# High parts first in every split product, and a new order of all steps (chunked attention with memory keys and a spatial-gating MLP, one core)

## The chip, the cores and the metric

The kernel runs on one core of one Trainium2 chip. The metric is device time in microseconds (us). The kernel before took 388.06 us, the median of three runs between 385.65 and 389.63 us.

Engines are named as in the profile: PE (matrix multiply; PEld is its weight load), DVE (vector), ACT (scalar functions), POOL (GpSimd), SP (the queue from which all loads and stores of data are issued).

## The reference

Attention in chunks of 32 tokens, each with 16 tokens to its left, 8 to its right and 8 memory keys; then an MLP whose gate mixes the tokens of a sequence:

```
for c in range(768 // 32):
    k_full = concat(mem_k, k[:, :, max(0, 32*c-16) : min(768, 32*c+32+8)])
    v_full = the same of v
    a = softmax(q_c @ k_full.T / 8);  out_c = a @ v_full
x = out, heads joined                       # 4 x 768 x 512
h = gelu(x @ w_in)                          # 4 x 768 x 1024
u, v = h[..., :512], h[..., 512:]
v_n = (v - mean) / sqrt(var + 1e-6) * g_ln
v_s = einsum('ts,bsd->btd', w_sg, v_n) + b_sg
result = x + (u * v_s) @ w_out
```

All inputs and the result are float32.

## The kernel before, in words

**Tiles.** Each of the 4 batches has 6 tiles of 128 tokens, 24 tiles in all, counted here from 0. Tiles 0, 1 and 2 are the first half of batch 0; a half of a batch has 384 tokens.

**Split products.** Every large operand is held as a high part (rounded to fp32r) and a low part (what is left). A product is made of three passes over its parts: low of one side with high of the other, high with low, high with high. `HL` (line 390) gives the order of the passes and `product` (line 392) issues them. A product's operands come in parts from other engines, so a pass can begin when its own parts are there.

**Steps.** The whole program is cut into named steps, each on one engine, and the long string `ORDER` (lines 32 to 80) lists all of them in the order in which they are recorded. Every engine runs its own steps in that order and waits where data or a buffer is missing; nothing overtakes. A star at a name takes the step's second engine. What the names mean, with tile u, batch b, half h, column block j:

- `q`, `k`, `v` + u: loads of a tile's queries, keys, values (SP); two buffers for q and k, three for v. `ri..`, `ro..`: loads of the pieces of w_in and w_out; `g` + two digits: loads of the pieces of w_sg.
- `d3`, `d2`, `d5`, `d6`, `d8`, `d9` + piece: turn 64-bit weights to float32 and split them (ACT, DVE, DVE, DVE, ACT, and POOL, DVE or ACT). `Xi1.` are PE steps that subtract the high part for four pieces of w_in. `ga`, `gb`: high and low part of w_sg (ACT; POOL or DVE).
- `S` u scores (PE), `mx`, `sb` largest and subtraction (DVE), `ex` exponential (ACT), `z` zeroes keys outside (POOL), `sm`, `sr` sum and reciprocal (DVE), `nm` normalisation (DVE or POOL), `T` transposes (PE), `p` their copy out of PSUM (ACT or DVE), `A` attention times values (PE), `xc`, `xh`, `xl` copy, high part and low part of the tile's result x (ACT, ACT, DVE or POOL).
- `V` b tile: x times the v half of w_in (PE, 12 matmuls of 512 columns), `v1` to `v9`: gelu, the layer norm and the split (the normalisation `v7` waits for the power `v6` on POOL). `U` b h j: x times the u half (12 matmuls of 384 columns), `u1` its gelu. `W`: the mix over tokens (18 matmuls), `w1` to `w4`: scale, gate, split. `O`: times w_out (12 matmuls), `o1` the sum with x, `out` the store.
- `zz` n: n matmuls on the identity, which compute nothing that is used.

A score step and a value step have 64 small matmuls each in the trace, with as many weight loads.

**What a reader needs from the code.** In before, the lines on which the change rests are these; the functions that issue them stand below:

```
HL = ((1, 0), (0, 1), (0, 0))
for a, c in HL:
    for lhs, rhs in parts:
        eng.matmul(ps, lhs(a), rhs(c), start=(k == 0), stop=(k == n - 1))
```

Part 0 is the high part, part 1 the low part; a is the part of the left operand, c of the right one.

## Time and profile before

| what | value |
|---|---|
| runs | 388.06 us median (385.65, 388.06, 389.63) |
| the profiled execution | 387.39 us, of which its span is 385.6 us |
| PE busy | 375.7 us, 97% of the span |
| DVE busy | 216.4 us, 56% |
| ACT busy | 154.1 us, 40% |
| POOL busy | 80.9 us, 21% |
| data moved | 43.95 MB |

The span goes from the first to the last instruction of the program; 1.8 us of the profiled execution lie around it. Busy is time in which an engine has an instruction in work. PE's matmuls overlap each other a little, so the length of a step is better read from the chain of waits, where each piece begins when the one before it ends.

### The profile page before, as it was taken

The numbers are of one execution on the slowest core, as the hardware profiler recorded it, in microseconds if no ns is written. First come the engines' busy times: TensorE is split into PE (matmuls) and PEld (weight loads), VectorE is DVE, ScalarE is ACT, GpSimd is POOL, SyncE is SP. The second block draws the span as 40 slices with busy tenths as digits, with TensorE's granted clock in tenths as the row PEclk, the third lists the DMA queues.
The fourth block names the chain that finished last, engine by engine and source line by source line (L and its number), as shares of the span: only waits on it lengthen the run. The fifth ranks groups of instructions, "written<-read, shape, count | busy, mean of one in ns | idle before, by whom it ended". The sixth has DMA issues, their size and how long they took to land.

```text
span 385.6 us, 10848 instructions
## 1 busy us (share of the span) xinstructions
PE 375.7 (97%) x4832; PEld 345.7 (90%) x4832; DVE 216.4 (56%) x404; ACT 154.1 (40%) x261; POOL 80.9 (21%) x100
## 2 busy tenths in 40 slices
PE   7979999999999999999999999999999999999996
PEld 3547988899999988899999989899999988999996
DVE  3799999999966365565345432531542414525522
ACT  3587799666531363463014341531210232511100
POOL 1003175223522201302005301420012133410010
PEclk9989999999999999999999999999999999999999
DMA  8999776756535246112002230000001110000022
GB/s 285 407 397 346 240 253 207 255 194 218 191 114 174 93 140 214 45 36 77 0 2 76 85 129 23 22 2 0 0 2 61 63 41 0 2 0 2 6 78 82
DMA packets 19150, 43.95 MB, mean 114 GB/s; under 512 B 2592, under 2 KB 8224, under 8 KB 19104
## 3 DMA queue, kind: packets, MB, share of 16 engines
q1 hardware_dynamic: 19104, 43.26, 31.8%
q8 instruction: 38, 0.62, 0.7%
q14 instruction: 8, 0.07, 0.1%
HBM read 36.96 MB, written 6.29 MB: 112 GB/s over the span
## 4 chain that ended last, share of the span: by engine, by line
PE 90%; DMA 3%; DVE 3%; ACT 2%; issue 1%; SPq 0%; ACTq 0%
PE mmd L92 22%; PE mmb L92 21%; PE mmc L92 19%; PE mma L92 19%; PE av L92 5%; PE s L92 4%; DMA ka<-in_ks 2%; DMA vb<-in_vs 1%; DVE w_sg_lo L92 0%; ACT L92 0%; SPq L92 0%; DVE pt L92 0%; ACT w_in_hi L92 0%; ACT pt L92 0%; ACT w_sg_hi L92 0%
## 5 line engine op out<-in xcount | busy, mean ns | idle before, releaser
L92 ACT ACT_TABLE_LOAD x20 | 25.7, 1283 | 3.6 <-DVE w_sg_lo L92 2.4
L92 DVE SCALAR_TENSOR_TENSOR mmd<-mmd,g_all,b_all 128x384 f32<-128x384 f32 x9 | 5.6, 620 | 15.7 <-PE mmd L92 15.7
L92 DVE SCALAR_TENSOR_TENSOR mmc<-mmc,g_all,b_all 128x384 f32<-128x384 f32 x8 | 5.0, 625 | 14.3 <-PE mmc L92 14.3
L92 PEld LDWEIGHTS av<-pt,vb 64*64 64x64 f32 x512 | 8.3, 134 | 4.2 <-issue 2.9
L92 PE MATMUL av<-pt,vb 64*64 64x32 f32 x512 | 9.3, 220 | 2.9 <-issue 2.1
L92 PEld LDWEIGHTS s<-kb,qb 64*32 64x32 f32 x768 | 8.7, 109 | 3.6 <-issue 1.7
L92 DVE SCALAR_TENSOR_TENSOR mmb<-mmb,g_all,b_all 128x384 f32<-128x384 f32 x9 | 5.6, 619 | 11.3 <-PE mmb L92 11.3
L92 PE MATMUL s<-ka,qa 64*32 64x64 f32 x768 | 10.5, 232 | 1.3 <-DMA ka<-in_ks 1.3
L92 PE MATMUL mmd<-w_in_hi,paira 128*128 128x512 f32 x40 | 11.7, 415 | 0.0
L92 PE MATMUL s<-kb,qb 64*32 64x64 f32 x768 | 10.8, 231 | 0.8 <-issue 0.8
L92 PEld LDWEIGHTS s<-ka,qa 64*32 64x32 f32 x768 | 8.7, 108 | 3.1 <-issue 2.0
L92 PE MATMUL mma<-ident 128*128 128x512 f32 (+1 forms) x16 | 9.9, 768 | 1.4 <-POOL mhalf L92 1.4
L92 PE MATMUL mmb<-w_in_hi,paira 128*128 128x512 f32 x40 | 11.0, 397 | 0.0
L92 PE MATMUL mmd<-w_in_hi,pairb 128*128 128x512 f32 x40 | 11.0, 396 | 0.0
L92 POOL TENSOR_TENSOR rsa<-rsa,mhalf 128x1 f32<-128x1 f32 x8 | 4.4, 551 | 28.2 <-DVE rsa L92 28.2
L92 DVE TENSOR_REDUCE mxa<-s 128x8 f32<-128x512 f32 x8 | 5.5, 684 | 8.2 <-PE s L92 8.2
L92 PEld LDWEIGHTS av<-pt,va 64*64 64x64 f32 x512 | 8.2, 135 | 1.8 <-issue 1.0
L92 POOL TENSOR_TENSOR paira<-xc,paira 128x512 fp32r<-128x512 f32 x4 | 5.5, 1410 | 19.8 <-ACT paira L92 19.8
L92 PEld LDWEIGHTS mmd<-w_in_hi,paira 128*128 128x128 f32 x40 | 7.8, 201 | 1.7
L92 PEld LDWEIGHTS av<-pt,vc 64*64 64x64 f32 x512 | 8.2, 135 | 1.3 <-issue 1.3
L92 PE MATMUL mma<-pairb,w_in_hi 128*128 128x384 f32 x48 | 9.3, 336 | 0.0
L92 PE MATMUL av<-pt,va 64*64 64x32 f32 x512 | 9.0, 220 | 0.1
(553 smaller groups left out, 1145.5 us busy)
## 6 DMA issues: line engine op xcount, KB each, us to landing
ka<-in_ks SPq DMA_DIRECT2D x12, 368.0 KB, 4.7
kb<-in_ks SPq DMA_DIRECT2D x12, 368.0 KB, 4.6
va<-in_vs SPq DMA_DIRECT2D x8, 512.0 KB, 4.6
vb<-in_vs SPq DMA_DIRECT2D x8, 512.0 KB, 4.9
vc<-in_vs SPq DMA_DIRECT2D x8, 512.0 KB, 5.2
qa<-in_qs SPq DMA_DIRECT2D x12, 256.0 KB, 4.2
qb<-in_qs SPq DMA_DIRECT2D x12, 256.0 KB, 4.5
out<-xa SPq DMA_DIRECT2D x8, 192.0 KB, 1.9
```

Of the source, the lines that this page charges most:

```text
L92: return self.tc.keep_in_program_order(getattr(self.engine, name)(*args, **kw))
```

## The change

The passes of all products begin with high times high. Which of the two mixed passes comes second depends on the product; for V of batch 0 it is the low part of x, with the low part of w_in last, and for U of batch 0 the other way. Within a pass the terms stand in the order in which their last part is made in `ORDER`. The number of matmuls is the same.

`ORDER` is new from its first to its last line. Of its 53 lines the diff shows two of the new ones, which hold V00 (the first V product), S3, A1, T2 and the loads of tiles 4 and 5.

```diff
@@ ORDER
 ...
+d3i03 v3 xl0 d8i11 d5i00 g50 Xi11 p1* g41 d6i00 S2 d9i11 d2i03 g21 d2i01 d3i02 d5i03 V00 d8i00 mx2 g31 d5i01 k4
+sb2 q4 d6i01 ex2 S3 d9i00* sm2 g40 d2i02 v100 sr2 d6i03 g10 d8i01 A1 nm2 k5 d8i03 d9i01* q5 T2 xh1 d9i03 mx3 g30
 ...
-    HL = ((1, 0), (0, 1), (0, 0))
-
-    def product(eng, ps, parts):
+    HL = ((0, 0), (0, 1), (1, 0))
+    LH = ((0, 0), (1, 0), (0, 1))
+
+    at = {name.rstrip("*"): i for i, name in enumerate(ORDER.split())}
+
+    def made(names):
+        names = list(names)
+        return sorted(range(len(names)), key=lambda i: at[names[i]])
+
+    def product(eng, ps, parts, order):
         n = 3 * len(parts)
         k = 0
-        for a, c in HL:
+        for a, c in order:
 ...
-                for kt in range(4)
-            ])
+                for kt in made(f"d9i1{kt}" for kt in range(4))
+            ], LH if b == 0 else HL)
 ...
-                for kt in range(4)
-            ])
+                for kt in made(f"d9i0{kt}" for kt in range(4))
+            ], HL if b == 0 else LH)
 ...
-                for st in range(6)
-            ])
+                for st in made(f"v9{b}{st}" for st in range(6))
+            ], HL)
 ...
-                for ft in range(4)
-            ])
+                for ft in made(f"w4{b}{h}{ft}" for ft in range(4))
+            ], LH)
```

What moves, engine by engine, at three places.

PE around the first V product. `s<-` are scores, `av<-` values, `<-ident,e` transposes, `w_in_hi,neg` an X step, `w_in..,paira 128x512` a V product. Before:

```order
L92 MATMUL s<-ka,qa 32x64 x32
L92 MATMUL av<-pt,vb 64x32 x32
L92 MATMUL mmb<-md,ident 128x512
L92 MATMUL mmb<-w_in_hi,neg 128x512
L92 MATMUL s<-kb,qb 32x64 x32
L92 MATMUL mmc<-ident,ec 128x128 x4
L92 MATMUL mmd<-w_in_hi,paira 128x512 x4
L92 MATMUL mmd<-w_in_lo,paira 128x512 x4
L92 MATMUL mmd<-w_in_hi,paira 128x512 x4
L92 MATMUL av<-pt,vc 64x32 x32
```

In the change, from the scores of tile 2 on:

```order
L92 MATMUL s<-ka,qa 32x64 x32
L92 MATMUL mmc<-w_in_hi,paira 128x512 x8
L92 MATMUL mmc<-w_in_lo,paira 128x512 x4
L92 MATMUL s<-kb,qb 32x64 x32
L92 MATMUL av<-pt,vb 64x32 x32
L92 MATMUL mmd<-ident,ec 128x128 x4
L92 MATMUL mma<-w_in_hi,paira 128x512 x8
L92 MATMUL mma<-w_in_lo,paira 128x512 x4
L92 MATMUL av<-pt,vc 64x32 x32
L92 MATMUL s<-kb,qb 32x64 x32
L92 MATMUL mmb<-ident,ed 128x128 x4
L92 MATMUL mmc<-w_in_hi,paira 128x512 x8
```

V00 stood behind A1, X13, S3 and T2 and now stands straight behind S2, ahead of those that remain (S3, A1, T2); S5 and T3 now stand ahead of V02.

SP, the queue of loads near its beginning (`raw.` are pieces of w_in). Before:

```order
L92 DMA rawc<-in_w_in 128x1024
L92 DMA qb<-in_qs 128x512
L92 DMA rawb<-in_w_in 128x1024
L92 DMA rawa<-in_w_in 128x1024
L92 DMA va<-in_vs 128x1024
L92 DMA vb<-in_vs 128x1024
L92 DMA vc<-in_vs 128x1024
L92 DMA rawd<-in_w_in 128x1024
L92 DMA qa<-in_qs 128x512
L92 DMA ka<-in_ks 128x736
```

In the change:

```order
L92 DMA kb<-in_ks 128x736
L92 DMA rawd<-in_w_in 128x1024
L92 DMA qb<-in_qs 128x512
L92 DMA va<-in_vs 128x1024
L92 DMA rawb<-in_w_in 128x1024
L92 DMA rawe<-in_w_in 128x1024
L92 DMA rawf<-in_w_in 128x1024
L92 DMA rawh<-in_w_in 128x1024
L92 DMA ka<-in_ks 128x736
L92 DMA qa<-in_qs 128x512
L92 DMA rawg<-in_w_in 128x1024
L92 DMA vc<-in_vs 128x1024
```

Seven of the eight pieces of w_in now stand ahead of the keys and queries of tile 2 (`ka`, `qa` in these rows), where four stood; the values of tiles 1 and 2 moved back.

POOL, after its zeroing of the first tile's keys. Before:

```order
L92 MEMSET ea 32x4x2x16
L92 TENSOR_TENSOR w_in_lo<-mh,w_in_hi 128x512
L92 TENSOR_TENSOR ed<-ed,rda 128x4x128
L92 TENSOR_TENSOR w_sg_lo<-uf,w_sg_hi 128x384
L92 MEMSET eb 32x4x2x8
```

In the change:

```order
L92 MEMSET ea 32x4x2x16
L92 TENSOR_TENSOR ea<-ea,rda 128x4x128
L92 TENSOR_TENSOR eb<-eb,rdb 128x4x128
L92 TENSOR_TENSOR w_in_lo<-mh,w_in_hi 128x512
L92 TENSOR_TENSOR rsa<-rsa,mhalf 128x1
L92 TENSOR_TENSOR w_in_lo<-mg,w_in_hi 128x512
L92 TENSOR_TENSOR vha<-ga,vha 128x512
L92 TENSOR_TENSOR w_sg_lo<-ua,w_sg_hi 128x384
```

The normalisations of tiles 0 and 1 came to POOL from DVE, and so did a second piece of w_in and a low part of the first V result.

## Rows read from the trace of the kernel before

**Rows 1.** The page, part 1: engine, busy us (share of the span), number of instructions.

```profile
PE 375.7 (97%) x4832; PEld 345.7 (90%) x4832; DVE 216.4 (56%) x404; ACT 154.1 (40%) x261; POOL 80.9 (21%) x100
```

**Rows 2.** Windows of 10 us of the span: us, busy us (instructions) of PE, PEld, DVE, ACT, POOL, then the granted clock of TensorE, the DMA share and GB/s.

```profile
20.00:30.00 10.00, 7.30 (x206) 5.39 (x205) 9.92 (x20) 7.45 (x14) 0.00 (x0) 0.83 1.04 394
30.00:40.00 10.00, 10.00 (x223) 7.96 (x223) 9.61 (x15) 8.67 (x16) 3.67 (x3) 1.00 0.95 333
90.00:100.00 10.00, 10.00 (x197) 9.72 (x198) 9.53 (x16) 4.46 (x8) 4.32 (x4) 1.00 0.34 131
340.00:350.00 10.00, 10.00 (x60) 10.00 (x59) 2.99 (x6) 1.52 (x3) 1.01 (x1) 1.00 0.00 0
```

**Rows 3.** The timeline of PE: start us, us, engine, line, operation, out<-in, count, idle time before it and what ended that. These are tile 1's values in two parts, S3, T2, and the first and the last pass of V00.

```profile
...
21.69 1.01 PE L92 MATMUL av<-pt,vb 64*64 64x32 f32 x55 [0.59 <-DVE paira L92]
24.81 0.32 PE L92 MATMUL av<-pt,vb 64*64 64x32 f32 x9 [2.11 <-issue]
...
26.47 1.19 PE L92 MATMUL s<-kb,qb 64*32 64x64 f32 x64
27.58 1.11 PE L92 MATMUL mmc<-ident,ec 128*128 128x128 f32 x4
28.35 1.73 PE L92 MATMUL mmd<-w_in_hi,paira 128*128 128x512 f32 x4
...
30.85 1.09 PE L92 MATMUL mmd<-w_in_hi,paira 128*128 128x512 f32 x4
```

**Rows 4.** The same of earlier steps: transposes of tile 1, scores of tile 2.

```profile
17.04 0.66 PE L92 MATMUL mmc<-ident,eb 128*128 128x128 f32 x4
20.24 0.86 PE L92 MATMUL s<-ka,qa 64*32 64x64 f32 x64
```

**Rows 5.** The chain of work that ended last: start us, us, what. The load of tile 0's keys, V02, a pair of score steps, a transposes step, a product of 384 columns (U or O), a lone score step, a V product behind value steps, a W product, and the last sum.

```profile
1.15 3.21 DMA ka<-in_ks
...
36.00 2.80 PE mmb L92 x12
38.80 1.45 PE s L92 x94
65.38 0.44 PE mmd L92 x4
120.71 2.08 PE mma L92 x12
138.50 0.79 PE s L92 x53
141.28 2.99 PE mmd L92 x12
182.74 3.12 PE mmb L92 x18
382.20 0.56 DVE xd L92
```

**Rows 6.** What PE waited for over the whole span: engine, tile, releaser: us in total, times, longest us.

```profile
PE av L92 <- issue: 2.1, 1, 2.1
PE s L92 <- DMA ka<-in_ks: 1.3, 2, 0.6
PE s L92 <- issue: 0.8, 1, 0.8
PE av L92 <- DMA vb<-in_vs: 0.2, 1, 0.2
```

**Rows 7.** The timeline of SP: when loads were issued. The next group has how long they took to land.

```profile
9.66 0.33 SPq L92 DMA_DIRECT2D rawg<-in_w_in  x1
17.03 0.33 SPq L92 DMA_DIRECT2D rawf<-in_w_in  x1
27.30 0.33 SPq L92 DMA_DIRECT2D ue<-in_w_sgT  x1
```

**Rows 8.** DMA issues of the first 30 us: tensor, count, KB each, us from issue to landing.

```profile
rawg<-in_w_in SPq DMA_DIRECT2D x1, 512.0 KB, 10.3
rawf<-in_w_in SPq DMA_DIRECT2D x1, 512.0 KB, 8.9
ue<-in_w_sgT SPq DMA_DIRECT2D x1, 192.0 KB, 5.4
```

**Rows 9.** The timeline of DVE and POOL: two shifts of weight pieces, a full-size operation, the low parts of two pieces of w_in, a small operation; on POOL a low part of w_in.

```profile
27.92 0.42 DVE L92 TENSOR_SCALAR mh<-mh 128x512 int32<-128x512 int32 x1
28.26 0.42 DVE L92 TENSOR_SCALAR mf<-mf 128x512 int32<-128x512 int32 x1
34.00 0.68 DVE L92 TENSOR_TENSOR paira<-av,paira 128x512 fp32r<-128x512 f32 x1
34.60 0.68 DVE L92 TENSOR_TENSOR w_in_lo<-mf,w_in_hi 128x512 fp32r<-128x512 f32 x1
35.26 1.73 DVE L92 TENSOR_TENSOR w_in_lo<-me,w_in_hi 128x512 fp32r<-128x512 f32 x1
36.91 0.19 DVE L92 RECIPROCAL rda<-rda 128x8 f32<-128x8 f32 x1
34.78 1.66 POOL L92 TENSOR_TENSOR w_in_lo<-mh,w_in_hi 128x512 fp32r<-128x512 f32 x1 [26.73 <-ACT w_in_hi L92]
```

**Rows 10.** The page, part 3: the queue that brings instructions: packets, MB, share of 16 engines.

```profile
q8 instruction: 38, 0.62, 0.7%
```

More of the change, by code (lines that the diff above doesn't have):

```diff
@@ L38 @@
-g11 d5i00 ro0 v100 V01 sm3 xh2 d6i00 d8i01 v5 xl2 d8i03 cb d8i00 d9i01* ro1 xc2 d9i03 V02 v101 d9i00* sr3 v501
-ga00 nm3* ga30 v500 ga50 gb00 vx01 ga21 S5 v102 S4 gb30* ga11 k7 mx5 ga20 q7 U002 ga51 k6 mx4 ga10 q6 sb5 g31
-sb4 g40 vx00 T3 v502 ex5 U000 p3* ex4 z5 vy00 sm5 v600 sm4 sr5 gb10* A3 sr4 nm5 u1002 nm4 S7 xc3 v6 v700 xh3 k9
-U003 mx7 ga31 q9 xl3 ga40 v800 gb51* T4 gb31 sb7 u1000 T5 p4 S6 gb40* g41 p5* g01 U001 mx6 q8 ex7 k8 vx02 vy01
-sb6 v601 vy02 sm7 ex6 v602 A5 v701 z6 ga41 sr7 sm6 v801 nm7* A4 v8 xc5 v702 ga01 xh5 gb41 sr6 v7 V03 xc4 v901*
@@ L78 @@
[L78 to L80 removed]
+q0 ri10 k0 ri12 k1 ri13 q1 v0 ri11 d3i10 ri00 d2i10 d5i10 ri01 zz10 S0 d6i10 d8i10 mx0 d3i12 ri03 zz2 Xi10 sb0
+k2 d2i12 ex0 d5i12 d9i10 z0 sm0 d3i13 q2 d6i12 ri02 zz5 S1 sr0 d2i13 d8i12 nm0* mx1 Xi12 v2 d5i13 T0 sb1 d9i12
@@ new lines @@
+d6i13 ex1 p0* d3i11 k3 sm1 d8i13 zz6 A0 d2i11 d3i00 q3 sr1 d5i11 Xi13 xh0 nm1* xc0 v1 d3i01 d2i00 T1 d9i13 d6i11
+d3i03 v3 xl0 d8i11 d5i00 g50 Xi11 p1* g41 d6i00 S2 d9i11 d2i03 g21 d2i01 d3i02 d5i03 V00 d8i00 mx2 g31 d5i01 k4
+sb2 q4 d6i01 ex2 S3 d9i00* sm2 g40 d2i02 v100 sr2 d6i03 g10 d8i01 A1 nm2 k5 d8i03 d9i01* q5 T2 xh1 d9i03 mx3 g30
+p2 xl1 V01 v4 xc1 sb3 d5i02 g00 v500 ro1 ex3 ro0 d6i02 cb A2 sm3 vx00 sr3 vy00 nm3 v600 v101 v700 d8i02 S5 v5
+v501 xh2 d9i02 T3 q7 mx5 xc2 k7 v800 xl2 V02 ga00 v900 sb5 ga50 p3* ga10 vx01 gb50 gb10* U000 g20 ex5 vy01 gb00*
@@ new lines @@
+g01 v601 ga30 g51 z5 ga40 v701 ga31 sm5 gb30 U001 gb31* g11 sr5 gb40* v102 nm5* v801 v502 U002 ga41 v901 vx02
+ga21 d3o0 ga20 gb41* u1000 vy02 gb20 T5 ga01 S4 ga51 gb21* ga11 A3 q6 mx4 gb01 d3o1 k6 u1002 gb11* S7 u1001 v6
+xc3 sb4 gb51 k9 U003 p5* xh3 q9 v602 mx7 xl3 ex4 A5 v702 sb7 sm4 v8 V03 d2o0 u1003 sr4 d2o1 xc5 nm4 d5o1 d5o0 T4
+ex7 d6o1 S6 p4 sm7 ro3 xh5 A4 q8 mx6 v802 k8 sr7 d8o1 xl5* v7 V05 xc4 v902 sb6 xh4 ex6 nm7 xl4 V04 v103 d6o0 z6
+d9o1 sm6 d8o0 ro2 v503 sr6 d9o0 vx03 v105 vy03 U012 v505 nm6* v104 vx05 vy05 v504 v605 U013 u1012 vx04 v603 v705
@@ new lines @@
+vy04 v703 v805 v604 v803 v905* S8 v903 u1013 d3o3 S9 q10 v704 k10 d3o2 U010 mx9 k11 v804 q11 mx8 v904 sb9 sb8
+W000 ex9 d2o2 ex8 d2o3 d5o2 sm8 sm9 u1010 sr8 d6o2 U011 nm8* sr9 w1000 d8o2 nm9 d9o2 w2000 T7 u1011 T6 p7 T9
+w3000 T8 d5o3 S10 p6* S11 w4000* k12 mx10 q12 A6 q13 mx11 k13 sb10 xc6 v9 W001 sb11 d6o3 p8* ex10 ex11 sm10 d8o3
+z11 W011 sr10 w1001 nm10* sm11 d9o3 w2001 sr11 w3001 nm11 W013 w4001 w1011 w2011 w3011 w4011 W012 w1013 w2013
+w3013 w4013* A7 w1012 w2012 S13 xc7 v10 p9* w3012 S12 mx13 k15 q15 w4012* W002 q14 mx12 k14 sb13 sb12 ex13 ex12
@@ new lines @@
+ex18 A12 p15* v16 xc13 z18 v812 sm18 v15 O010 p14 v912 sr18 xc12 nm18 O012 o1010 out010 S19 o1012 out012 A15
+mx19 k21 sb19 q21 p17 O013 v18 ex19 sm19 sr19 O011 nm19* o1013 out013 V10 o1011 xh11 xh10 out011 xl11* xh9 xl10
+xl9* U113 v110 v510 xc15 vx10 vy10 U111 v610 u1113 v710 v810 v910* U102 u1111 V15 u1102 T18 v115 S20 v515 S21
+k22 mx20 q22 vx15 V13 mx21 q23 k23 sb20 sb21 ex20 vy15 ex21 v615 sm20 sm21 A14 sr20 v715 nm20* sr21 v113 S22 v17
+xc14 nm21 V11 v815 p16* v513 mx22 v915* U110 vx13 sb22 v111 vy13 v511 v613 vx11 v713 vy11 ex22 A17 v611 v813
@@ new lines @@
+sm22 A16 v913 v20 v19 U112 v711 u1110 xc16 sr22 p18* v811 nm22 xc17 v911* V14 u1112 T22 v114 T20 T21 v514 T19
+vx14 S23 p19 vy14 v614 A18 mx23 v714 A19 sb23 v21 v814 p20* v914 v22 W103 ex23 p21 z23 sm23 sr23 nm23* W113
+w1103 w2103 U100 w1113 w2113 w3113 w4113* W111 u1100 W100 w1111 w2111 w3111 w4111* W110 w1100 w2100 U101 w1110
+w2110 w3110 w4110* W102 w3100 u1101 w4100* w3103 w4103* W101 w1102 w2102 w3102 w4102* W112 w1101 w2101 w3101
+w4101* O101 w1112 w2112 w3112 w4112 O110 o1101 out101 O113 o1110 out110 O102 o1113 out113 O103 o1102 out102 O100
@@ L81 @@
+out303 O311 o1302 out302 O300 o1311 out311 o1300 out300
 """
```

63 lines of the change are left out of this document (20 added, 43 removed).

## The prediction

> **What bounds the kernel now.** First the page: PE is busy for 375.7 of 385.6 us [rows 1]. Busy PE can hide waits, so next the list of what PE waited for: over the whole span it names few, and the longest, 2.1 us, lies at the start [rows 3, 6]. The windows show where PE falls short of full: it has 7.30 of 10 us between 20 and 30, and then 10.00 of 10 in the later stretches shown [rows 2]. So the kernel has two parts. From the first V product (V00) on, PE runs almost without a gap to the end, and its work there is fixed: a V product takes 2.80 us, U 2.08, W 3.12 [rows 5]. Before V00, at 28.35 us [rows 3], PE waits for others, or works on the identity: it has by then done four score steps, two value steps, three transposes and four X steps. The time is set by how early the dense part begins, and by the few gaps in it.
>
> What filled the start is in PE's timeline [rows 3]: A1 began at 21.69 behind a wait for DVE, broke off, and went on at 24.81 after 2.11 us in which no semaphore held it ("issue"). PE was slower afterwards: S3, T2 and the first pass of V00 took 1.19, 1.11 and 1.73 us, where others of their kind took 0.86, 0.66 and 1.09 [rows 3, 4], and the window has a granted clock of 0.83, so PE was for a part of it at the lower of its two levels, 1.2 GHz instead of 2.4 [rows 2]. DVE is the second bound. It is 9.92, 9.61 and 9.53 of 10 us busy in the windows from 20, 30 and 90 us; only later does it sink to 2.99 [rows 2]. An order that gives PE its work sooner must therefore also get DVE there sooner.
>
> **The change, step by step.** No product gets a matmul more or less, so a pass order costs nothing by itself. What it gives is slack: V00 may begin with the high parts alone, and the low part of x is wanted only after a third of it (2.80 / 3 = 0.93 us), the low part of w_in after two thirds.
>
> *Up to V00.* V00 no longer stands behind A1, X13, S3 and T2, but behind S2. The keys and queries of tile 2 now stand behind seven pieces of w_in. Summing the KB in the new queue order, tile 2's queries end at 5,968 KB. In before that point was reached by the load of piece g: 9.66 + 10.3 = 19.96 us [rows 7, 8]. S2 then takes 0.86 [rows 4], and X11 waits for ACT at about the same time, so V00 begins at about 21.5 instead of 28.35. That is not yet gain: what stood ahead of it is only done later. Tile 1's values now end at 8,128 KB, reached at 17.03 + 8.9 = 25.9 us [rows 7, 8], so A1 waits for them whatever PE does.
>
> *Up to V02*, where both orders can be compared. PE's side: V02 now stands behind S5 and T3. Tile 5's queries end at 11,040 KB. In before the load of w_sg into ue ended at 10,736 KB and 27.30 + 5.4 = 32.7 us [rows 7, 8]; the 304 KB left take 0.8 at the 394 GB/s of the windows [rows 2]. So S5 can begin at 33.5; with S5 0.79 and T3 0.44 [rows 5], V02 begins at 34.75 and wants the low part of tile 2's x at 35.7.
>
> DVE's side: up to that low part (xl2) it now has 55 instructions: 40 of full size, 8 shifts, 6 small ones and one normalisation. Back to back they start 0.60 us apart (34.00 to 34.60), shifts 0.34 (27.92 to 28.26), and a small one adds about 0.12, the normalisation about 0.46 (estimates from the overlap of 0.08 between neighbours) [rows 9]. That is 24.0 + 2.7 + 0.7 + 0.5 = 27.9 us. It begins when the first piece of w_in is there and ACT has read it: the piece ends at 768 KB. In before 624 KB were there when tile 0's keys landed, 1.15 + 3.21 = 4.36 us [rows 5]; 144 KB more take 0.4, and with the starts between engines and one ACT operation of some 0.7 I let DVE start at 5.7 (an estimate). Without a wait it is done at 33.6. I allow 1.3 us for waits on S0, S2, S5 and the exponentials, and one collision with POOL: with POOL at work on a low part of w_in, DVE's own low part took 1.73 us and not 0.68, so 1.05 more [rows 9]. The new order sets a POOL step on w_in exactly where DVE normalises tile 2. Sum: 35.95. V02 thus does its first pass, waits 0.25 us, and ends at 35.95 + 1.87 = 37.8.
>
> In before V02 ended at 38.80 [rows 5], without S5 and T3; with them the same progress stood at 38.80 + 0.79 + 0.44 = 40.03. So **PE is 2.2 us earlier at V02**. Ends: with loads 1.1 us sooner and neither collision nor more than 0.7 of waits, V02 begins at 33.75 and ends at 36.55, 3.5 earlier; with four collisions it is later than before (below).
>
> *From V02 to the end.* The same steps in other places. DVE gets air: the first W product stands behind ten score steps where it stood behind sixteen, so DVE has fewer softmaxes to do before it. Three later gaps of before, 0.6 (one of the two waits on ka), 0.8 and 0.2 us [rows 6], need not come back, but others may: between a full gain of 1.6 and a loss of 2 I take 0.5, nearer to the gain, because windows like the two from 30 and 340 us show that this kind of order leaves few gaps [rows 2]. A product behind a score or value step costs 0.2 more than one behind a product (2.99 against 2.80) [rows 5]; there are 17 such places from V00 on, where there were 20, and three more transposes behind small steps: 0.4 gained. The tail is the same: a last sum of 0.56 [rows 5] and a store. The passes of W and O begin with high parts, so a late low part does less harm; nothing waits for it in before, so I give that no time. POOL and ACT are far from full [rows 1].
>
> Sum against the profiled execution: 387.39 - 2.2 - 0.5 - 0.4 = **384.3 us**. The median of the runs is 388.06, 0.7 above that execution; 384.3 is 1.0% under the median. About 1% is what a measurement of this kernel can tell from no change, that is 384.2 to 391.9.
>
> **Two rules against the change.** On DVE and POOL the row shows one collision of 1.05 us [rows 9]. The Trainium skill, "GPSIMD Engine Reference", section "Specifications", says that POOL shares its SBUF interfaces with the vector engine and that the two contend when the vector instruction has two SBUF inputs. By that rule all four meetings of the first rival below would cost DVE, and the sum would be 387.5 instead of 384.3; the 1.73 us agrees with it.
>
> On the fetch of instructions the rows show 38 packets [rows 10], about one for every 254 of PE's 9,664 matmuls and weight loads [rows 1], and a PE that stood still for 2.1 and 0.8 us without a releaser [rows 6]. The Trainium skill, "Runtime: NRT & Kernel Launch", section "Instruction fetch mechanics", says that the next block is fetched while the current one runs, and that the cost of crossing into it is mostly hidden. By that the fourth rival below would have no price; the trace disagrees, with 2.1 us.
>
> **Rivals.**
> 1. *DVE pays for POOL each time* (chance 0.12). The normalisations of tiles 0 and 1 and two low parts of w_in now run on POOL ahead of xl2: four collisions of 1.05, so xl2 at 33.6 + 1.3 + 4.2 = 39.1 and V02 ends at 41.0, 1.0 later than before. Time 387.39 + 1.0 - 0.9 = 387.5. For it: the 1.73. Against it: much of DVE's work beside those steps reads PSUM or one operand.
> 2. *The clock falls once more* (0.12). PE now has its gaps ahead of X11, T2 and S5. After the gap of before S3, T2 and the first pass of V00 cost 0.33, 0.45 and 0.64 us more than such steps at the higher level [rows 3, 4], 1.4 in all. If that comes behind S5, where nothing absorbs it, the time is 384.3 + 1.4 = 385.7. For it: the waits I find are 1 to 2 us long. Against it: in the windows shown from 30 us on the clock is at 1.00 [rows 2], gaps of 0.6 and 0.8 notwithstanding.
> 3. *The gain is given back to DVE before the W products* (0.08). DVE is full up to 100 us [rows 2]; if V05 waits for the low part of its x, the 2.2 us go and 387.0 remains. For it: that low part and PE would meet within half a microsecond in the new order.
> 4. *Slower: PE's instructions come late* (0.09). A score or value step is 128 instructions in one microsecond, so two of them eat one packet. In before that struck once under full DMA, at 22.7 us, and cost 2.11 us and the 1.4 of the slow clock after it, 3.5. The new order has S, A and S steps side by side while loads run, three at a time in several places. One late packet with its clock gives 387.8, two give 391.3, three 394.8: the change is slower from the second on. For it: the "issue" rows; against it: by 90 us DMA is at 0.34 [rows 2], and in before only one further packet was late, by 0.8.
> 5. *Better* (0.14): loads a microsecond sooner and no collision, 3.5 us at V02, and all of the old gaps gone: 387.39 - 3.5 - 1.6 - 0.4 = 381.9.
>
> The forecast has the remaining 0.45, spread from 383 to 385.5. That V00 did not move at all is excluded by the order of PE; that moving it yields nothing is rival 3.
>
> **The numbers.** 384.3 us. From 381.5 to 388.2 lie the forecast, the first three rivals, most of the fifth, and one late packet; more late packets are left out. Faster by over 1% is half of the forecast and rival 5 with a little on either side: 0.40. Slower by over 1% needs three late packets, or two and another rival: 0.05. Within 1%: 0.55.
>
> **What would show it.** V00 at 21 to 22.5 us in PE's timeline, and A1 behind a DMA wait at about 26. S5 at 33.5, behind the queries of tile 5. V02 ending at 37 to 38.5, with a short wait on DVE inside it. DVE's normalisation of tile 2 or the low part next to it at over 1.2 us instead of 0.68 would show the collision. From V02 on, PE's waits should come to under 2 us. I am wrong if V02 ends after 40, if a window behind 34 us has a granted clock under 0.95, or if "issue" waits of PE come to more than 3 us.

## The result, and the profile after

The changed kernel took 389.76 us (median of 20 runs, 387.73 to 393.80) where the kernel before, beside it, took 388.22 (385.44 to 390.51). The ratio is 1.0053, with a 95% interval from 1.0032 to 1.0073. Two later comparisons gave 1.0078 [1.0043, 1.0113] and 1.0087 [1.0054, 1.0121]. So the change makes the kernel slower by 0.5 to 0.9%, some 2 to 3.4 us; by the medians alone it is 1.5, 2.0 and 2.5 us in the three. The forecast was 384.3, which is 3.8 under before's median. The profiled execution took 390.92 us, with a span of 389.0.

The page, part 1, of the changed kernel answers to [rows 1]: engine, busy us (share of the span), instructions.

```profile
PE 375.0 (96%) x4828; PEld 344.5 (89%) x4828; DVE 220.9 (57%) x405; ACT 152.5 (39%) x256; POOL 90.7 (23%) x106
```

PE's busy time is the same to 0.7 us, and the span is 3.4 us longer: what came are waits. POOL has 9.8 us more and DVE 4.5 more, although DVE has one instruction more only. The windows, in the columns of [rows 2]:

```profile
20.00:30.00 10.00, 8.44 (x213) 5.92 (x214) 10.00 (x19) 7.01 (x12) 0.85 (x1) 1.00 1.02 375
30.00:40.00 10.00, 8.70 (x158) 6.36 (x157) 9.28 (x21) 9.45 (x15) 5.32 (x5) 1.00 0.94 316
90.00:100.00 10.00, 10.00 (x235) 9.62 (x234) 5.99 (x11) 1.97 (x5) 1.02 (x1) 1.00 0.28 92
```

PE now has its gaps spread over both of the first windows, and the granted clock is 1.00 where it was 0.83. At 90 us DVE is no longer full (5.99 where [rows 2] had 9.53). PE's timeline where [rows 3] stood shows V00 (its first eight matmuls), S3 in two parts, A1, S5, T3, V02 in three parts:

```profile
22.25 2.13 PE L92 MATMUL mmc<-w_in_hi,paira 128*128 128x512 f32 x8
...
25.52 0.69 PE L92 MATMUL s<-kb,qb 64*32 64x64 f32 x45 [0.20 <-DVE ec L92]
27.26 0.41 PE L92 MATMUL s<-kb,qb 64*32 64x64 f32 x19 [1.05 <-issue]
27.60 1.14 PE L92 MATMUL av<-pt,vb 64*64 64x32 f32 x64
...
33.85 0.86 PE L92 MATMUL s<-kb,qb 64*32 64x64 f32 x64
35.15 0.63 PE L92 MATMUL mmb<-ident,ed 128*128 128x128 f32 x4 [0.44 <-ACT gb L92]
36.20 1.20 PE L92 MATMUL mmc<-w_in_hi,paira 128*128 128x512 f32 x4 [0.42 <-ACT paira L92]
37.84 1.20 PE L92 MATMUL mmc<-w_in_hi,paira 128*128 128x512 f32 x4 [0.44 <-DVE paira L92]
38.88 1.09 PE L92 MATMUL mmc<-w_in_lo,paira 128*128 128x512 f32 x4
```

V00 did come 6 us earlier. V02 ends at 39.97, though, and the same progress stood at 40.03 in before. The list of PE's waits answers to [rows 6] (us in total, times, longest us):

```profile
PE s L92 <- DMA ka<-in_ks: 2.7, 2, 1.8
PE mma L92 <- POOL mhalf L92: 1.3, 1, 1.3
PE av L92 <- issue: 1.2, 1, 1.2
PE s L92 <- issue: 1.1, 1, 1.1
PE av L92 <- ACT pt L92: 0.9, 1, 0.9
PE av L92 <- ACT xc L92: 0.7, 1, 0.7
```

One of the waits for `ka` (1.8) is S0 at the start, and the second row is the wait of PE's first instruction. The others, with S3's 1.05 already shown, stand in the timeline at A4, A10, S18 and inside A18:

```profile
57.77 1.14 PE L92 MATMUL av<-pt,vb 64*64 64x32 f32 x64 [0.89 <-ACT pt L92]
...
111.59 1.14 PE L92 MATMUL av<-pt,vb 64*64 64x32 f32 x64 [0.68 <-ACT xc L92]
...
126.93 0.86 PE L92 MATMUL s<-ka,qa 64*32 64x64 f32 x64 [0.91 <-DMA ka<-in_ks]
...
180.69 0.82 PE L92 MATMUL av<-pt,va 64*64 64x32 f32 x41
182.69 0.49 PE L92 MATMUL av<-pt,va 64*64 64x32 f32 x20 [1.18 <-issue]
```

That is 3.7 us behind V02, where before had waits of 0.6, 0.8 and 0.2 [rows 6].

### The profile page after: what moved, and what is told of

It is laid out like the page before. It is cut to its first block, busy times and chain, and to the rows that moved or that the text cites. A ratio compares the mean times of both kernels' runs of the same rounds, so it can differ in the third digit from the quotient of the medians.

```text
span 389.0 us, 10857 instructions
## 1 busy us (share of the span) xinstructions
PE 375.0 (96%) x4828; PEld 344.5 (89%) x4828; DVE 220.9 (57%) x405; ACT 152.5 (39%) x256; POOL 90.7 (23%) x106
## 4 chain that ended last, share of the span: by engine, by line
PE 82%; DMA 11%; ACT 3%; SPq 1%; issue 1%; POOL 0%; DVE 0%
PE mmb L92 22%; PE mmd L92 19%; PE mma L92 17%; PE mmc L92 17%; PE av L92 5%; PE s L92 3%; DMA rawg<-in_w_in 3%; DMA qb<-in_qs 2%; DMA uc<-in_w_sgT 2%; DMA ua<-in_w_sgT 2%; DMA g_all<-in_g_ln 2%; SPq L92 1%; DMA ka<-in_ks 1%; ACT L92 1%; ACT w_sg_hi L92 0%
## 5 line engine op out<-in xcount | busy, mean ns | idle before, releaser
L92 DVE SCALAR_TENSOR_TENSOR mmb<-mmb,g_all,b_all 128x384 f32<-128x384 f32 x9 | 5.6, 621 | 16.4 <-PE mmb L92 16.4
L92 DVE SCALAR_TENSOR_TENSOR mma<-mma,g_all,b_all 128x384 f32<-128x384 f32 x9 | 5.6, 625 | 15.9 <-PE mma L92 15.9
L92 PE MATMUL mmb<-pairb,w_out_hi 128*128 128x384 f32 x56 | 12.3, 342 | 0.0
L92 POOL TENSOR_TENSOR pairb<-ue,pairb 128x384 fp32r<-128x384 f32 x2 | 2.1, 1026 | 41.2 <-ACT pairb L92 41.2
L92 ACT CAST pairb<-uh 128x384 fp32r<-128x384 f32 x4 | 2.1, 514 | 24.0 <-DVE uh L92 24.0
L92 PE MATMUL mma<-w_in_hi,paira 128*128 128x512 f32 x40 | 11.0, 399 | 0.0
L92 PE MATMUL mmb<-w_in_hi,pairb 128*128 128x512 f32 x40 | 10.8, 396 | 0.0
L92 PEld LDWEIGHTS mmb<-pairb,w_out_hi 128*128 128x128 f32 x56 | 9.7, 188 | 0.1
L92 PE MATMUL mmc<-w_in_hi,paira 128*128 128x512 f32 x32 | 8.9, 404 | 0.9 <-DVE paira L92 0.4
L92 POOL TENSOR_TENSOR rsa<-rsa,mhalf 128x1 f32<-128x1 f32 x8 | 5.0, 621 | 19.7 <-DVE rsa L92 19.7
L92 POOL TENSOR_TENSOR rsc<-rsc,mhalf 128x1 f32<-128x1 f32 x8 | 4.4, 548 | 21.9 <-DVE rsc L92 21.9
```

The lines of the kernel that those rows point to most:

```text
L92: return self.tc.keep_in_program_order(getattr(self.engine, name)(*args, **kw))
```

## The experiments

Three theories were set against each other. **G (gaps):** the passes cost nothing, the head gains little, and the new order has new waits of PE further on. **P (passes):** the pass order or the sorted terms cost time. **H (head):** the first 40 us are worse. Later came **M (waits move on):** a wait taken out opens the next one, and **C (the one execution):** the profile that the forecast was built on was not a usual one. The ratios below are to the kernel before, run in turn with each kernel on the same chip.

### Order and passes apart

The old order with the new passes:

```diff
 ORDER = """
-q0 ri10 k0 ri12 k1 ri13 q1 v0 ri11 d3i10 ri00 d2i10 d5i10 ri01 zz10 S0 d6i10 d8i10 mx0 d3i12 ri03 zz2 Xi10 sb0
+q0 k0 k1 ri12 q1 ri11 ri10 v0 v1 zz5 S0 v2 mx0 ri13 sb0 ex0 z0 d3i12 q2 sm0 zz12 S1 k2 d2i12 sr0 d5i12 d3i11
...
```

> The order of before with the new passes and the sorted terms. Three theories stand for the 2 us that the change costs. Theory G (gaps): up to V02 the new order gains nothing, because DVE's chain is as late as before, and from 50 us on its steps stand so that PE waits more often than in before; the passes cost nothing. Theory P (passes): the new passes or the order of the terms cost time at each product. Theory H (head): something in the first 40 us is worse and is carried to the end. Here G and H expect before +-0.5 us (ratio 0.9987 to 1.0013); at best 0.5 us is gained, where V00 no longer waits for a low part first. P expects before + 1.5 to + 2.5 us.

Measured: ratio 1.0004 [0.9967, 1.0040]. G and H expected this; the least that P expected, 1.5 us or 1.004, lies at the edge of the interval. The new order with the old passes:

```diff
-    HL = ((0, 0), (0, 1), (1, 0))
-    LH = ((0, 0), (1, 0), (0, 1))
+    HL = ((1, 0), (0, 1), (0, 0))
+    LH = HL
...
-        return sorted(range(len(names)), key=lambda i: at[names[i]])
+        return range(len(names))
```

> The new order with the old passes (low parts first), which also takes the sorting of the terms away. The low part of tile 2's x is now wanted at the first matmul of V02 and not after its first pass. G and H: V02 begins at about 37.8 us and ends at 40.6, 0.7 to 1.5 us later than in the changed kernel, so before + 2.3 to + 3.5 us (ratio 1.006 to 1.009). P: before +-0.5 us, since the passes were the cost.

Measured: 1.0192 [1.0142, 1.0242], a loss of 1.9% where G and H expected 0.6 to 0.9% and P none. With both runs P falls. V01 and V02 each wait for the low part of x before they begin, as the timeline of PE shows (the rows are the first of V01 and of V02):

```profile
29.57 1.20 PE L92 MATMUL mma<-w_in_hi,paira 128*128 128x512 f32 x4 [0.84 <-DVE paira L92]
...
36.69 1.20 PE L92 MATMUL mmc<-w_in_hi,paira 128*128 128x512 f32 x4 [1.62 <-DVE paira L92]
```

In its profile more followed at V05, S22 and V30 (0.4 to 0.5 each) and a stop of 0.9 without a releaser inside A9, and after the stop inside A18 the clock fell (last section). The new order needs the new passes; in the old order they change nothing that can be measured.

### The old head

The order of before up to V02, then the new one:

```diff
 ORDER = """
-q0 ri10 k0 ri12 k1 ri13 q1 v0 ri11 d3i10 ri00 d2i10 d5i10 ri01 zz10 S0 d6i10 d8i10 mx0 d3i12 ri03 zz2 Xi10 sb0
+q0 k0 k1 ri12 q1 ri11 ri10 v0 v1 zz5 S0 v2 mx0 ri13 sb0 ex0 z0 d3i12 q2 sm0 zz12 S1 k2 d2i12 sr0 d5i12 d3i11
...
```

> The new passes, the order of before up to V02, and the new order for all that follows. H: the loss lay in the head, so the time is that of before, +-0.6 us. G: V02 ends where it does in before, and what the new order costs comes after it: before + 1.3 to + 3 us (ratio 1.003 to 1.008), with PE waits of 0.7 us or more at A4, at A10 and at S18 as in the changed kernel. The 1.2 us behind S23 (A18, with no releaser) may move, since fewer identity matmuls stand ahead of it in one order than in the other.

Measured: 1.0305 [1.0258, 1.0353]. This run tells nothing about H. At the seam T5 waited 6.0 us for a normalisation on POOL, a wait that neither kernel has, and the clock fell behind it. It is used in the last section only; on H the profiles further down have to answer.

### Mending the gaps

Three steps moved (three pieces of the order):

```diff
-T4 ex7 d6o1 S6 p4 sm7
+T4 p4 ex7 d6o1 S6 sm7
...
-v11 A10 nm15 xc9 v12 p11* xc10 v13 O003
+v11 O003 A10 nm15 xc9 v12 p11* xc10 v13
...
-xh7 S18 out002 xl8* xh6 q19 xl7 mx17 V12 q20
+xh7 out002 xl8* xh6 q19 xl7 mx17 V12 S18 q20
```

> The changed kernel with three steps moved in the order: the copy of tile 4's transposes (p4) stands ahead of tile 7's exponential on ACT; the product O003 stands ahead of the value step A10; the scores of tile 18 stand behind the product V12 instead of ahead of it. G: the waits of 0.9 us (A4), 0.9 us (S18) and about 1 us (A10) go, and with them 1.5 to 2.7 us: before -0.8 to + 0.6 us (ratio 0.998 to 1.0015). H and P: the time stays at before + 1.3 to + 2.5 us, because something else (DVE, or PE itself) sets the pace and the waits move on.

Measured: 1.0156 [1.0099, 1.0214], slower than the change itself. The waits at A4, A10 and S18 are gone, but V05 behind A4 now waits twice. PE's timeline of that run, V05:

```profile
57.65 1.19 PE L93 MATMUL mmc<-w_in_hi,pairb 128*128 128x512 f32 x4 [1.03 <-ACT pairb L93]
60.08 1.20 PE L93 MATMUL mmc<-w_in_hi,pairb 128*128 128x512 f32 x4 [1.24 <-DVE pairb L93]
61.12 1.10 PE L93 MATMUL mmc<-w_in_lo,pairb 128*128 128x512 f32 x4
```

ACT stood behind a table load for tile 7's exponential, and DVE's low part of tile 5 met POOL (last section). T17 waits 0.8 us as well, for tile 17's normalisation on DVE. In this execution the granted clock also fell, to 0.78 between 25 and 30 us and 0.88 in the next 5. So M holds at A4, and at S18 if T17's wait is what came in its place; in A10's place no new wait came. Four kernels mended more carefully. One puts a product between the small steps S23 and A18:

```diff
-p19 vy14 v614 A18 mx23
+p19 U100 vy14 v614 A18 mx23
...
-W103 ex23 p21
+W103 u1100 ex23 p21
...
-U100 w1113
+w1113
```

> The changed kernel with one product (U100) moved from behind W113 to between S23 and A18, and its gelu before tile 23's exponential. In the changed kernel, and in the three kernels of this study that keep its end, PE stood still for about 1.2 us inside A18 with no releaser, where S23 and A18 follow each other. Theory G (the gaps of the new order cost what it loses, each can be mended by itself): with 2 us of product between them the packet of instructions is there in time; the gap at A18 goes, and the time is 1.0 to 1.4 us under the changed kernel, before + 0.3 to + 1.0 us (ratio 1.001 to 1.0025). Rival M (waits move on): the gap comes back at the next pair of small steps or at W103, and the time stays at before + 1.3 to + 2.5 us.

Measured: 1.0048 [1.0023, 1.0072], above what G said, and within M's range. The stop inside A18 is gone, though, and none came elsewhere; PE's timeline shows the last matmuls of U100, then A18 and A19, with no wait:

```profile
179.69 0.86 PE L93 MATMUL mmb<-paira,w_in_hi 128*128 128x384 f32 x4
180.48 1.14 PE L93 MATMUL av<-pt,va 64*64 64x32 f32 x64
181.44 1.11 PE L93 MATMUL av<-pt,vb 64*64 64x32 f32 x64
```

The second takes the late mends of the run before and moves DVE's maximum of tile 18 behind that normalisation, the third the place at 55 us, and the fourth takes all of it and moves one shift on DVE out of POOL's way. Their edits:

```diff
-v11 A10 nm15 xc9 v12 p11* xc10 v13 O003
+v11 O003 A10 nm15 xc9 v12 p11* xc10 v13
...
-V12 q20 k19 k20 xl6* sb17 mx18 ex17 U103 z17 sm17 sr17 v112 nm17
+V12 S18 q20 k19 k20 xl6* sb17 ex17 U103 z17 sm17 sr17 v112 nm17 mx18
```

> The changed kernel with O003 ahead of A10, and with the scores of tile 18 behind V12 instead of ahead of it; DVE's maximum of tile 18 now stands behind the normalisation of tile 17, so that it holds nothing up. G: the waits at A10 (0.7 to 1 us) and S18 (0.9 us) go and none takes their place; 1.5 to 1.9 us under the changed kernel, before -0.2 to + 0.5 us. M: T17 or another step waits instead; before + 1 to + 2.5 us.

```diff
-ex7 d6o1 S6 p4 sm7 ro3 xh5
+p4 xh5 ex7 d6o1 S6 xl5* sm7 ro3
...
-            ], LH if b == 0 else HL)
+            ], LH if b == 0 and tt < 3 else HL)
```

> The changed kernel with three things about 55 us changed: on ACT the copy p4 and the high part of tile 5's x (xh5) stand ahead of tile 7's exponential; on DVE tile 5's low part (xl5) stands ahead of tile 7's sum; V03 to V05 take the low part of x in their last pass. In the run with three mends only p4 was moved, and V05 then waited 1.0 us for xh5 and more for xl5. G: the wait at A4 (0.9 us) goes, V05 does not wait, and where the head was early (V02 ending at 38.4 us, as in that run) the early time is kept too: 0.9 to 2.4 us under the changed kernel, before -0.9 to + 0.6 us. M: DVE and ACT are full until 65 us and hand the wait to V04 or U012: before + 1.3 to + 2.5 us.

```diff
-d2i00 T1 d9i13 d6i11 d3i03 v3 xl0 d8i11
+T1 d9i13 d6i11 d2i00 d3i03 v3 d8i11 xl0
```

> All moves of the last three kernels together, and on DVE the shift of the weight piece 00 one step later, behind the last step of piece 11, out of the way of POOL's normalisation of tile 1 (the shift took 1.27 us there instead of 0.42). G: the sum of the gaps, 0.9 + 0.8 + 0.9 + 1.2 = 3.8 us under the changed kernel, and up to 1.5 more from the head: before -1.5 to -3.5 us (ratio 0.991 to 0.996), faster than both kernels. M: before +-1 us, since each mended gap opens another.

Measured: 1.0092 [1.0055, 1.0129], 1.0102 [1.0070, 1.0134] and 1.0063 [1.0033, 1.0093]. All three are slower than G said. In their profiles the mended waits are gone, but T17 still waits 0.8 us in the two with the late mends, so DVE's maximum of tile 18 was not the reason, and V04 waits 0.5 in the two with the mends at 55 us; in the last, S16 stops for 0.5 without a releaser. The ways from V02's end to the last O (here and below: to the end of PE's work, less 2.08 us for that O) are 342.0, 342.6 and 341.9 us. None is told apart from the change, whose ratios are 1.0053 to 1.0087. A last kernel of this kind is made to remove those two as well (two of its pieces):

```diff
-xh4 ex6
+xh4 ex7 ex6
...
-T16 v512 u1103 T17 T15 vx12 vy12 T14
+T15 v512 u1103 T14 T16 vx12 vy12 T17
```

> All moves of the run with all mends, and two more against the waits that they opened: on ACT tile 7's exponential goes behind the high part of tile 4's x (V04 waited 0.46 us for that), with DVE's sum and normalisation of tile 7 behind it; the transposes of tiles 15 and 14 go ahead of those of 16 and 17 (T17 waited 0.8 us). Theory G (separate waits): the way from V02's end to the last O falls from 343.2 to 339 to 340.5 us, and the time is 2.5 to 4 us under the changed kernel of the same call, ratio 0.994 to 1.000 to before. Theory M (each opens the next): the way stays at 341.5 or more, the ratio at 1.003 or more.

Measured: 1.0049 [1.0023, 1.0074], beside 1.0087 [1.0054, 1.0121] for the change in the same comparison. The way from V02's end to the last O is 340.7 us, just above what G said, with new waits of 0.5 us at T9 and at O010. The time is 1.1 us under the change by the medians, where G said 2.5 to 4, and not under before: by the way nearly G, by the ratio M.

### More profiles of both kernels

One execution is one draw. Both kernels were profiled again, unchanged.

> The kernel before, unchanged, for another profile of it and for the spread of the comparison. Theory C (the one execution): the execution on which the forecast was built held chance events (2.1 us at A1 with no releaser, the clock that fell after it, 1.1 us at S21) that most executions of this kernel don't have or have elsewhere; a profile without them ends PE's dense part 1.5 to 3 us earlier, at 379.5 to 381, and V02 with S5 and T3 stands before 39.5 us. Theory M (waits move on, the head does not carry through): those events are absorbed by the wait for DVE behind them, V02 stands at 39.5 to 40.1 as before, and the end stays at 381.5 to 383. Ratio to itself: 0.997 to 1.003.

> A third profile of the kernel before: the same numbers as for the second are looked for. C: events of 1 us or more with no releaser in at most one of the two new profiles ahead of V00; M: no matter how many, V02 with S5 and T3 stands at 39.5 to 40.1.

> The changed kernel, unchanged, on the same chip as the run beside it and as a yardstick for the kernels with mended gaps (ratios 1.0048 to 1.0102). Expected: ratio 1.003 to 1.008; the wait inside A18 of 1 to 1.2 us is there again, V02 ends between 38.4 and 40 us, and the waits at A4 or V05 and at A10 and S18 are there. C and M differ in where it loses: C expects PE's way from the end of V02 to the end to be as long as in the first profile of the changed kernel (343 us from V02's end to the last O, 3 more than before); M expects it to be longer by as much as V02 ends earlier.

> A third profile of the changed kernel: as for the second. If the way from V02's end to the last O is 343 us +-0.7 in all three profiles whatever V02's end, C holds; if the sum of V02's end and that way is the same (383 +-0.7) while V02's end moves by over 1 us, M holds.

> The changed kernel again, beside the three others: ratio 1.004 to 1.008; V02's end at 38.2 to 40 us, and 343.0 to 343.5 us from there to the last O, whatever V02's end.

Measured: before 0.9993 [0.9958, 1.0029] to itself; the change as told above. In all three profiles of before PE stops inside A1 and the window from 20 us has 0.83 of the clock. In the profile of its order with new passes, and in that of V00 alone (next section), A1 is not stopped and the clock stays at 1.00; there PE waits for DVE at T2 (2.35 us) or for the weights at V00 (0.5).

That does not make the fall of the clock the rule for before. Every execution has its mean granted clock on record, and it is 0.994 to 0.996 in the three that were profiled. Of 121 executions of before in the later comparisons, 48 have 0.999 or 1.000, and these have a mean span of 384.2 us; the other 73 have 386.0. Of the change's 39 executions 12 have 0.999 or 1.000 and a mean of 387.4 us, the others 388.3. So four in ten of before's executions hold next to no fall and are 1.7 us shorter, which is C's size (1.5 to 3 us); whether A1 stops in them no profile shows. Without a fall the change is 3.1 us longer than before, with one 2.3. The numbers that were set for before's profiles fit neither theory: the same progress as V02's end in the change stood at 40.7 and 40.5 us, where C said under 39.5 and M at most 40.1.

For the change, the way from V02's end to the last O was 343.2, 343.0 and 343.4 us in the first three profiles while V02's end moved by 1.7 us, as C says. The fourth, with 341.4, missed what was expected (343.0 to 343.5).

The second profile of before, A1 in PE's timeline:

```profile
22.08 1.01 PE L92 MATMUL av<-pt,vb 64*64 64x32 f32 x55 [0.61 <-DVE paira L92]
25.45 0.32 PE L92 MATMUL av<-pt,vb 64*64 64x32 f32 x9 [2.37 <-issue]
```

In the change the stop inside S3 is there every time too, but the head differs between executions. The third profile of the change, the three parts of V02:

```profile
34.49 1.18 PE L92 MATMUL mmc<-w_in_hi,paira 128*128 128x512 f32 x4 [0.18 <-ACT paira L92]
36.13 1.20 PE L92 MATMUL mmc<-w_in_hi,paira 128*128 128x512 f32 x4 [0.46 <-DVE paira L92]
37.17 1.10 PE L92 MATMUL mmc<-w_in_lo,paira 128*128 128x512 f32 x4
```

The same two waits inside V02's way, for ACT and for DVE, 1.7 us earlier than in the first profile. V02 ended at 39.97, 38.48, 38.26 and 40.14 us in the four. To see where each order loses time, one sum over PE's timeline helps: the time up to a point, less the work done by then, with 2.79 us for a V, 2.085 for a U, 3.12 for a W, 2.08 for an O, 1.25 for an X step, 0.44 for transposes, 0.72 for scores, 1.0 for values, and nothing for the identity. What is left is what PE lost so far:

| lost by PE up to | 40 us | 104 | 135 | 178 | 190 | end |
|---|---|---|---|---|---|---|
| before, profile 1 | 18.1 | 21.3 | 21.9 | 23.8 | 23.8 | 25.3 |
| before, 2 | 18.9 | 21.5 | 21.9 | 23.3 | 23.3 | 24.7 |
| before, 3 | 18.6 | 22.9 | 23.5 | 25.1 | 25.1 | 26.3 |
| change, profile 1 | 18.1 | 21.3 | 24.4 | 25.9 | 27.7 | 28.4 |
| change, 2 | 16.6 | 19.7 | 22.9 | 24.3 | 26.1 | 26.7 |
| change, 3 | 16.4 | 20.3 | 22.9 | 24.4 | 26.2 | 26.9 |
| change, 4 | 18.3 | 20.2 | 23.0 | 24.5 | 26.1 | 26.7 |
| U100 between | 16.9 | 19.4 | 22.0 | 23.5 | 23.9 | 24.5 |
| all mends and more | 16.2 | 19.2 | 21.5 | 23.1 | 23.4 | 24.1 |

On average the new order is 1.2 us ahead at 40 us and 1.5 at 104, so H falls. The three executions of before all hold a fall of the clock, however; in the two profiles of its order without one (new passes, and V00 alone) PE had lost 17.8 and 17.2 us at 40, where the change's mean is 17.4, and 25.9 and 25.1 at the end. Between 104 and 135 us the new order loses 2.9 where before loses 0.5, and between 178 and 190 us 1.7 where before loses nothing. Behind that it is 0.7 better. The sum is 1.75 us at the end of PE's work. From there to the end of the span it is 3.8 us in each profile of the change and 3.4 in each of before. That 0.37 lies behind the landing of the last store, from which it is 1.32 us to the last instruction in the change and 0.95 in before; why was not found. Together that is 2.1, the difference of the mean spans (387.8 and 385.7).

### V00 alone, and the two orders joined

V00 alone moved, in the old order with the new passes, and the same with S8 and S9 later:

```diff
-d9i13 d2i03 T2 d2i01 g50 mx3 p2 V00 k5
+d9i13 d2i03 V00 T2 d2i01 g50 mx3 p2 k5
```

> The order of before with the new passes and one move: V00 stands ahead of tile 2's transposes (T2) and not behind them. If the head's gain comes from V00 standing early (theory V): V00 begins at about 25.7 instead of 28.5 us, waits at most 0.7 us for the last low part of w_in, and V02 ends at 37.0 to 37.6 instead of 38.4; 0.7 to 1.4 us under the old order with new passes, unless S8's wait for its keys takes it back: ratio 0.996 to 1.000. If the head is set by DVE (theory D): V01 or V02 waits as much longer for the low parts of x, V02 ends at 38 to 38.6, ratio 0.998 to 1.002.

```diff
-xl5* S8 xl4 S9 k10 u1003 q10 v902* U013 k11
+xl5* xl4 u1003 v902* U013 S8 S9 k10 q10 k11
```

> The same, and the scores of tiles 8 and 9 with the loads of tile 10 behind U013 instead of ahead of it, since S8 waited 0.6 to 1.3 us for its keys in the profiles of the old order. V: that wait goes and V00's gain is kept, 1.3 to 2.4 us under before, ratio 0.994 to 0.997. D: the head gives nothing, S8's wait 0.6 at most: ratio 0.997 to 1.001. M: S10 or S11 waits for the later keys instead, ratio 0.999 to 1.003.

Measured: 0.9999 [0.9960, 1.0037] and 1.0097 [1.0057, 1.0137]. In the first V00 stood where forecast and V02 ended at 37.69 instead of 38.38, just above the 37.0 to 37.6 that V said; its timeline (V00 in three parts, A2):

```profile
25.71 2.12 PE L93 MATMUL mmc<-w_in_hi,paira 128*128 128x512 f32 x8
27.68 0.86 PE L93 MATMUL mmc<-w_in_lo,paira 128*128 128x512 f32 x3
29.08 0.50 PE L93 MATMUL mmc<-w_in_lo,paira 128*128 128x512 f32 x1 [0.54 <-ACT w_in_lo L93]
...
30.75 1.14 PE L93 MATMUL av<-pt,vc 64*64 64x32 f32 x64 [0.73 <-ACT pt L93]
```

Whether the 0.7 us reach the end can't be told, since the interval holds both. In the second S11 waited 1.9 us for its queries, whose load had moved back with S9: M again. A1 stopped for 2.4 us in that profile and V00 began only at 28.4, so it says nothing on V. Last, the new order up to tile 11's values and the old one behind, once plain and once with the mended first part:

```diff
 T13 w1010 T12 A11
-w2010 p12 w3010 S16 w4010 xc11 p13* v14 mx16 q18
-O000 k18 sb16 ex16 O002 sm16 o1000 sr16 out000 nm16* S17
+w2010 S17 w3010 k19 w4010 q19 p12* mx17 T14 sb17 ex17 z17 A12
+xc11 v14 p13* sm17 p14 v15 sr17 nm17 S16 mx16 k18 q18
...
```

> The new passes, the new order up to the value step of tile 11 (118 us), and the order of before for all that is left; behind the seam the copy of tile 12's transposes stands ahead of tile 17's maximum, and tile 19's scores with the loads of tile 21 stand behind O000, so that no small steps pile up there. Theory G (the loss lies in the second part of the new order): PE loses 20 to 21 us up to 118 us as in the changed kernel, then 3.0 to 3.8 as in the old order, and the dense part ends at 380 to 381.5: 1.5 to 3 us under the changed kernel, ratio 0.996 to 1.001. Theory M (whatever is gained early is waited for later): 5 us or more are lost behind 118 us, ratio 1.003 or more.

> The same with the first part of the kernel with all mends and more (c1), which had lost 19.9 us at 118 us where before had lost 21.6 to 23.4. G: dense part at 378.5 to 380, 2 to 3 us under before, ratio 0.992 to 0.997. M: ratio 0.999 or more.

Measured: 1.0048 [1.0014, 1.0082] and 1.0022 [0.9997, 1.0047]. In the first, PE lost 20.8 us up to 118 us as G says and 2.5 from 135 us on; but at the seam, where A12 and S16 stand side by side, a stop without a releaser came, as at A18:

```profile
119.37 1.14 PE L92 MATMUL av<-pt,va 64*64 64x32 f32 x64
120.43 0.64 PE L92 MATMUL s<-ka,qa 64*32 64x64 f32 x39
122.14 0.43 PE L92 MATMUL s<-ka,qa 64*32 64x64 f32 x25 [1.06 <-issue]
```

Behind 118 us it lost 4.6 in all, between G's 3.8 and M's 5. The second lost 20.9 and 3.9, with a stop of 0.8 inside S16; PE's work ended at 381.7, where G said 380 at most, so G's gain did not come. No version was found that beats the kernel before.

## Why the prediction was wrong

**V00 at about 21.5, X11 and S2 ahead of it: right.** 20.7 to 22.4 us in four profiles. A1 did not wait for its values, as forecast, but for S3, which stopped for 1.05 us ahead of it; it began at 26.4 to 27.8, near the 25.9 forecast, at which its values did land (25.1 to 26.0). S5 at 33.5: 32.9 to 34.0.

**DVE's side, 35.95 us, and V02 at 37.8: right in two executions of four, too early in the two others.** The low part of tile 2's x ended at 36.1 and 36.3 in two, at 37.8 and 38.0 in the others, and V02 ended 2.2 us behind it instead of 1.87. The mis-sized term is the allowance of 1.3 us for DVE's waits. DVE began at 5.5 to 5.7 as forecast (5.7), but tile 0's scores wait for its keys, which now stand behind the first piece of w_in: S0 began at 6.1 and 6.2 us in the good executions, at 7.2 and 7.8 in the others. Up to that low part DVE stood idle for 0.9 and 1.3 us in the good ones and for 2.1 and 2.6 in the others; in the fourth execution a second collision with POOL came on top (1.31 us for a shift, last section). DVE's timeline of the first profile, the maximum of tile 0:

```profile
9.00 0.69 DVE L92 TENSOR_REDUCE mxa<-s 128x8 f32<-128x512 f32 x1 [1.53 <-PE s L92]
```

So the 2.2 us at V02 were 1.2 on average: V02 stands at 39.2 in the change, and the same progress of before at 40.4 (three profiles, 40.0 to 40.7).

**The collision: right in size, wrong in place.** One was charged with 1.05 at tile 2's normalisation; none was there. It came at a shift, with 0.85 in each of the four profiles (last section).

**"From V02 to the end": the step that failed.** A gain of 0.5 from gaps and 0.4 from fewer changes between kinds of steps was forecast. The way from V02's end to the last O got 3.0 us longer (342.7 against 339.8 on average, before's without S5 and T3). The bound for a loss was 2 us, and the reason for taking a value near the gain, that later windows of the old order show full PE, says nothing about a new order of all steps: each place where two or three small steps meet had to be looked at by itself. Four such places held the loss: A10 behind A9 (0.7 us in every profile), S18 right behind S17, ahead of its keys (0.6 to 1.0), A18 behind S23 (0.9 to 1.2), and A4 behind ACT's exponential (0.9 and 1.0, in two profiles). They are readable from the order beforehand: a value step two places behind the one whose result still has to be copied out of its buffer (A8, A10), a score step whose load may only be issued when the score step two tiles earlier is done (S16, S18). The sum by kinds did not bear out the 0.4 either: from V02 on, the change's O steps took 65.8 us where before's took 64.9, its U steps 67.4 where they took 68.2. The term also counted sixteen score steps ahead of before's first W product; by the order there are fifteen.

**"The tail is the same": no**, by 0.37 us. With these averages the forecast's sum reads 387.39 - 1.2 + 3.0 + 0.4 = 389.6, against a median of 389.76.

**Rivals.** DVE paid for POOL (rival 1) once or twice before xl2 in each execution, with 0.85 to 0.9 for a shift, and not four times with 1.05. The clock, rival 2, did not fall in any of the four profiles of the change, where 0.12 was given. Its mean is 0.996 or less in 25 of the change's 39 recorded executions, though, so it does fall in many that were not profiled; where in them is not known. In the profiles of the experiments it fell between 25 and 35 us in four (three mends, all mends, V00 with S8 later, the first joined order). Late packets, rival 4, came as described, one inside S3 and one inside A18, but cost 0.9 to 1.3 us each and not 3.5: no slow clock followed. S3's delays V02 little, since V02 waits for DVE behind it anyway. Rival 3 (the gain is given back to DVE before the W products) did not come; at 104 us the new order is still 1.5 us ahead. Its time was also summed wrongly: 384.3 + 2.2 is 386.5, not 387.0. Rival 5 did not come either: V02 was at most 2.2 us ahead of before's mean. Only two or more late packets at the price of 3.5 would have ended beyond 388.2; a loss by several waits of 0.7 to 1.2 us behind 100 us was in no case.

**Still open.** That taking these waits out shortens the way is shown (U100 between: 340.5 us; all mends and more: 340.7). Why the times of those kernels are still not under before is shown in part. Their one profile each ended PE's work at 381.4 and 380.9 us, 1 us under the mean of before's three, but in executions with a granted clock of 0.998 and 0.999. Before's three held the fall, and of its 26 executions with a span under 384 us, which pull its median down, 24 have a clock of 0.999 or more and none was profiled. In the comparison with all mends and more, executions with at least 0.999 have mean spans of 384.4 us (before, 12), 387.2 (the change, 2 only) and 385.6 (all mends and more, 5). So the mends take back about 1.6 of 2.8 us, and where the other 1.2 lie is open.

## What to carry to other kernels

When an order of all steps is replaced, cost it place by place to the end: for each value, score or transpose step, what is it waiting for in the new order, and is a product between it and the step of its own kind ahead of it. A gain in the head is worth what the last of these places leaves of it. And take a second profile before building a sum on differences of 1 us: between executions of one kernel V02 moved by 1.9 us. Look at the granted clock of all executions as well: the forecast was built on one with a fall, which four in ten don't have.
